# w1's last 64 rows: half by a transfer with an outermost dimension of 4, half by one of 16

## Chip, cores, metric

One core of one Trainium2 chip. The metric is the device time of one execution in microseconds (us), lower is better. Before: 213.92 us.

## The reference, cut to what matters

The result is the sum of the layernormed input, an attention block over a sliding window of a cache and a small MLP block. The change touches one product of the MLP block, `layernorm(x) @ w1`, with 576 rows of w1.

```python
def _B_ref(x, w1, w2, w3, w4):
    B, S, D = x.shape                      # 4, 1, 576
    h = _gelu(_layernorm(x, axis=-1) @ w1) # w1 is 576 x 576
    ...                                    # shifts, @ w2, residual, layernorm, @ w3, gelu, @ w4
x = A_x
xn = _layernorm(x, axis=-1)
return x + _A_ref(xn, ...) + _B_ref(xn, ...)
```

## The kernel before: the parts that matter

576 rows are 4 x 128 and a rest of 64. The 512 rows fill 128 partitions; the 64 of w1 lie in 16 partitions, 4 rows in each, and those of w2 in 32 partitions, 2 rows in each. One queue, SP's, loads all weights and the cache in a fixed order, about 88 MB.

```python
w1rag = w4_t[0:16, 18 * D:22 * D]
w2rag = w4_t[0:32, 22 * D:24 * D]
...
# order in the queue: w2, wq, wq/w3 rest ("wqr"), the two ragged pieces ("r12"), w3, w1, 16 K tiles, 8 V tiles, wo, w4
ev_r12 = add_dma([(w1rag, B_w1[512:576, :].rearrange("(b a c) n -> a b (c n)", b=4, a=4)),
                  (w2rag, B_w2[512:576, :].rearrange("(b a c) n -> a b (c n)", b=4, a=8))], "r12", (), -58.5)
ev_w3 = add_dma([(w3_t[:], B_w3[0:512, :].rearrange("(p r) n -> p (r n)", r=4))], "w3", (), -57)
...
# in ln_ops, second layernorm: the last 64 columns, in the order of the rows in w1rag
r_out = ragsrc[:, idx, 0:64].rearrange("q (c a b) -> q c a b", c=4, a=4)
r_in = r_in.rearrange("q (b a c) -> q c a b", b=4, a=4)
add("dve", lambda e: e.tensor_copy(out=r_out, in_=r_in), waits=[f"{tag}_n", "rag_zero"], sig=tag, key=k0 + 0.05)
...
# pe_h: 4 matmuls over 128 partitions, then 4 over 16
for c in range(4):
    ins = e.matmul(HTps[h], lhsT=xn2T[0:16, 4 + c, :], rhs=w1rag[:, c * D + HALF * h:c * D + HALF * (h + 1)], start=False, stop=(c == 3))
```

The outermost dimension of the HBM side, the source (4 for w1's rest, 8 for w2's), is there on purpose: a 4 went with 4 of the 16 DMA engines and an 8 with 8. In the trace of this kernel four strings of packets hold the packets of 4608 bytes of w1's rest, four in each, eight hold those of 2304 bytes of w2's, and the semaphore of the two gets 12 single updates, from 16.61 to 17.80 us: 4 and 8 engines. A semaphore is a counter; in the program each transfer adds 16 to it. In the trace that is several updates, for w3 16 of them from 27.44 to 28.73 us, and the matmuls that wait for w3 start at 28.78, after the last.

## Time and profile before

| | before |
|---|---|
| median of 6 runs, us (lowest, highest) | 213.92 (213.80, 214.04) |
| span of the traced run | 212.7 |
| DMA queue, share of 16 engines | 97.6% |
| last update of w3's semaphore | 28.73 |
| last update of the last piece of w4 | 210.47 |
| from there to the last update of the stores of the result | 2.20 |

PE is TensorE (PEld its weight loads), DVE VectorE, ACT ScalarE, POOL GpSimd; SP issues the transfers. The span is what the trace shows from the first to the last instruction; the device time is longer by about 1.3 us. In the timeline each line has the start, the length, the engine, the source line, the operation, and in brackets the idle time before it and what ended it.

### The profile page before, as it was taken

Reading aid. Unit: us, or ns where it says so; the run is one execution under the profiler, and the core shown is the slowest. Engines: PE = TensorE matmul, PEld = TensorE weight load, DVE = VectorE, ACT = ScalarE, POOL = GpSimd, SP = SyncE. Lnnn points to the kernel's source line nnn. Section 1 sums busy time; section 2 is a strip of 40 time slices with the busy share of each in tenths; the row PEclk is TensorE's granted clock in tenths of the full one; section 3 lists DMA queues with packets and bytes.
Section 4 is the critical chain, followed back from the end, with each engine's and each line's share of the span. In section 5 each row is a group of like instructions: output and inputs, shape, how many; then the busy total and the mean of one; then the engine's idle time right before and its main releaser. Section 6 shows DMA issues by size and latency. Waiting matters only on the chain. (4 is left out here: it accounts for less than half of the span.)

```text
span 212.7 us, 4936 instructions
## 1 busy us (share of the span) xinstructions
PE 169.3 (80%) x2171; PEld 131.9 (62%) x2171; DVE 106.6 (50%) x162; ACT 61.6 (29%) x76; POOL 15.4 (7%) x55
## 2 busy tenths in 40 slices
PE   0038359999999999999997095999999696779964
PEld 0013246888778887888874044888878575657532
DVE  0332700676766666666664429877776473600100
ACT  2001204566555666666666520000000000000000
POOL 8300000450000000000000000000000000000000
PEclk9999958999999999999999679999999999969999
DMA  7999999999999999999999999999999999999993
GB/s 290 414 390 467 437 401 431 425 433 410 434 431 428 425 428 438 421 425 434 422 450 456 404 434 438 413 462 410 431 441 419 425 450 419 449 409 421 429 407 119
DMA packets 5150, 88.65 MB, mean 417 GB/s; under 512 B 600, under 2 KB 740, under 8 KB 1300
## 3 DMA queue, kind: packets, MB, share of 16 engines
q1 hardware_dynamic: 5124, 88.49, 97.6%
q8 instruction: 8, 0.13, 0.2%
q14 instruction: 2, 0.02, 0.0%
q10 hardware_dynamic: 16, 0.01, 0.0%
HBM read 88.49 MB, written 0.00 MB: 416 GB/s over the span
## 5 line engine op out<-in xcount | busy, mean ns | idle before, releaser
L370 DVE COPY kt<-ps 128x1024 bf16<-128x1024 bf16 x80 | 52.3, 687 | 26.1 <-PE ps L363 25.9
L363 PEld LDWEIGHTS ps<-perm_bf,ring 128*128 128x128 bf16 x1024 | 57.5, 98 | 9.6 <-issue 9.2
L363 PE MATMUL ps<-perm_bf,ring 128*128 128x128 bf16 x1024 | 62.1, 219 | 0.8
L369 ACT ACTIVATE kt<-ps 128x1024 bf16<-128x1024 bf16 x48 | 48.8, 1023 | 30.1 <-PE ps L363 29.0
L441 DVE TENSOR_TENSOR kt<-PT,mU_bf 128x2048 bf16<-128x2048 bf16 x32 | 38.7, 1223 | 17.9 <-PE ps L452 17.9
L452 PE MATMUL ps<-ring,kt 128*128 128x256 bf16 x256 | 29.8, 280 | 5.1 <-PEq L621 5.1
L452 PE MATMUL ps<-w,kt 128*128 128x256 bf16 x256 | 28.4, 272 | 4.8 <-PEq L621 4.8
L452 PEld LDWEIGHTS ps<-ring,kt 128*128 128x128 bf16 x256 | 25.6, 100 | 9.2 <-issue 5.6
L452 PEld LDWEIGHTS ps<-w,kt 128*128 128x128 bf16 x256 | 24.8, 98 | 8.3 <-issue 5.5
L466 ACT ACTIVATE Ov<-ps 64x128 f32<-64x128 f32 x2 | 0.5, 272 | 68.2 <-PE ps L452 68.2
L377 PE MATMUL ps<-kt,Qs 128*32 128x512 bf16 x272 | 17.8, 382 | 1.4 <-PEq L621 1.4
L299 PE MATMUL ps<-ident_bf,xn_bf 4*128 4x4 bf16 x8 | 0.6, 170 | 12.7 <-DVE ragsrc L293 12.7
L398 POOL COPY Qs<-Qpad 128x128 bf16<-128x128 bf16 x16 | 4.6, 293 | 82.1 <-PE ps L377 68.2
L377 PEld LDWEIGHTS ps<-kt,Qs 128*32 128x32 bf16 x272 | 5.7, 95 | 6.8 <-issue 1.5
L416 PE MATMUL ps<-kt,sel 128*128 128x512 bf16 x16 | 5.0, 480 | 5.6 <-ACT kt L408 5.6
L299 PEld LDWEIGHTS ps<-ident_bf,xn_bf 4*128 4x128 bf16 x8 | 0.4, 112 | 12.7 <-issue 10.3
L560 PE MATMUL ps<-w,x1nT 128*32 128x387 bf16 (+7 forms) x90 | 5.8, 400 | 2.7 <-DMA w<-in_B_w_dram 2.5
L416 PEld LDWEIGHTS ps<-kt,sel 128*128 128x128 bf16 x16 | 1.8, 117 | 8.8 <-ACT kt L408 6.1
L560 PEld LDWEIGHTS ps<-w,x1nT 128*32 128x32 bf16 x90 | 4.5, 124 | 3.9 <-DMA w<-in_B_w_dram 2.6
L597 DVE CAST out_sb<-ps 4x288 bf16<-4x288 f32 x1 | 0.4, 445 | 12.7 <-PE ps L479 12.7
L466 DVE COPY Ov<-ps 64x128 f32<-64x128 f32 x2 | 0.6, 283 | 10.4 <-PE ps L452 10.4
L479 PE MATMUL ps<-w,h2T_sb 128*4 128x288 bf16 x54 | 3.6, 286 | 2.1 <-DMA w<-in_B_w_dram 2.1
(113 smaller groups left out, 73.7 us busy)
## 6 DMA issues: line engine op xcount, KB each, us to landing
ring<-in_A_k_cache_dram SPq DMA_DIRECT2D x16, 2048.0 KB, 14.4
w<-in_A_v_cache_dram SPq DMA_DIRECT2D x4, 4096.0 KB, 23.4
ring<-in_A_v_cache_dram SPq DMA_DIRECT2D x4, 4096.0 KB, 31.2
w<-in_B_w_dram SPq DMA_DIRECT2D x1, 4608.0 KB, 24.1
w<-in_A_wo_dram SPq DMA_DIRECT2D x1, 4608.0 KB, 32.0
kt<-in_A_wq_dram SPq DMA_DIRECT2D x1, 4096.0 KB, 13.1
w<-in_B_w_dram SPq DMA_DIRECT2D x1, 2592.0 KB, 29.2
w<-in_B_w_dram SPq DMA_DIRECT2D x3, 576.0 KB, 14.0
```

What stands on the lines that cost most here:

```text
L299: e.transpose(XTps[idx][:, r, :], v[:, r, :], ident_bf[0:B, 0:B])
L363: ins = e.transpose(tb[n % 4][:, t, :], slot_t(c)[:, 8 * k + t, :], perm_bf[:])
L369: return "act", lambda e: e.activation(out=ktbuf[:, n % 16], in_=tb[n % 4], func=ACTF.Copy)
L370: return "dve", lambda e: e.tensor_copy(out=ktbuf[:, n % 16], in_=tb[n % 4])
L377: ins = e.matmul(Sps[32 * u:32 * u + 32, q, :].rearrange("p (t i) -> p t i", t=16), lhsT=Qs[:, c % NPOS, 32 * u:32 * u + 32], rhs=ktgrp[:, ...
L398: P(lambda e, c=c, cc=cc: e.tensor_copy(out=Qs[:, c % NPOS, :], in_=Qpad_t[:, 128 * cc:128 * cc + 128]), waits=["qT", "qs_zero"] + ([f"SC{ ...
L416: ins = e.matmul(ps[:, 4 + g, :].rearrange("p (q t) -> p q t", q=4), lhsT=sel[:, g // 2, g % 2, i, :], rhs=P_v[:, i], start=(i == 0), stop ...
L441: return lambda e: e.tensor_tensor(out=pads[:, j], in0=PTv[:, b, q, VQ * j:VQ * (j + 1), :].unsqueeze(2).to_broadcast([128, VQ, 32, 2]), i ...
L452: ins = e.matmul(Ops, lhsT=pads[:, j, t:t + 2].rearrange("p t h e -> p (t h e)"), rhs=vslot[q][:, t0:t0 + 2 * Dh], start=(q == 0 and j == ...
L466: add(eng, (lambda e, o_=o_, i_=i_: e.activation(out=o_, in_=i_, func=ACTF.Copy)) if x else (lambda e, o_=o_, i_=i_: e.tensor_copy(out=o_, ...
L479: return e.matmul(ACC[h], lhsT=lhsT, rhs=rhs, start=start, stop=stop, tile_position=(0, 32 * h), skip_group_check=True)
L560: ins = e.matmul(H2ps[k][32 * g:32 * g + 32, :].rearrange("p (x c) -> p x c", c=9)[:, :, off:off + cnt], lhsT=x_, rhs=w[:, base_:base_ + 1 ...
```

## The change

Its intent is balance among the DMA engines. The four that carry all 64 rows have more bytes than the others (four packets of 4608 bytes more on each); half of the rows now go by all 16. A second copy on DVE puts the activations of that half into the matching order.

```diff
-        ev_r12 = add_dma([(w1rag, B_w1[512:576, :].rearrange("(b a c) n -> a b (c n)", b=4, a=4)),
+        ev_r12 = add_dma([(w1rag[:, 0:2 * D], B_w1[512:544, :].rearrange("(b a c) n -> a b (c n)", b=4, a=4)),
+                          (w1rag[:, 2 * D:4 * D], B_w1[544:576, :].rearrange("(p c) n -> p (c n)", c=2)),
                           (w2rag, B_w2[512:576, :].rearrange("(b a c) n -> a b (c n)", b=4, a=8))], "r12", (), -58.5)
...
             if idx == 1:
-                r_out = ragsrc[:, idx, 0:64].rearrange("q (c a b) -> q c a b", c=4, a=4)
-                r_in = r_in.rearrange("q (b a c) -> q c a b", b=4, a=4)
+                r_sp = r_in[:, 32:64].rearrange("q (p c) -> q c p", c=2)
+                add("dve", lambda e: e.tensor_copy(out=ragsrc[:, idx, 32:64].rearrange("q (c p) -> q c p", c=2), in_=r_sp),
+                    waits=[f"{tag}_n", "rag_zero"], sig=None, key=k0 + 0.045)
+                r_out = ragsrc[:, idx, 0:32].rearrange("q (c a b) -> q c a b", c=2, a=4)
+                r_in = r_in[:, 0:32].rearrange("q (b a c) -> q c a b", b=4, a=4)
```

## The prediction

> **What bounds the kernel now.** I read the page's summary of all engines first (parts 1 to 3), then the chain of work that ended last, then the timeline of the first 20 us, where the change lies, and last the packet and semaphore records under these views.
>
> ```profile
> span 212.7 us, 4936 instructions
> PE 169.3 (80%) x2171; PEld 131.9 (62%) x2171; DVE 106.6 (50%) x162; ACT 61.6 (29%) x76; POOL 15.4 (7%) x55
> ...
> DMA  7999999999999999999999999999999999999993
> ...
> q1 hardware_dynamic: 5124, 88.49, 97.6%
> q8 instruction: 8, 0.13, 0.2%
> q14 instruction: 2, 0.02, 0.0%
> ```
>
> No compute engine is full, but the 16 DMA engines are busy from the first slice to the last but one: 88.49 MB on one queue take 97.6% of 16 engines' span. The reader should also note the two small "instruction" rows: ten packets of program text that share these engines. They matter below.
>
> ```profile
> 177.53 7.16 PE ps L452 x64
> 184.69 0.02 issue
> 184.71 24.68 DMA ring<-in_B_w_dram
> 209.39 0.04 issue
> 209.43 1.42 PE ps L479 x18
> 210.85 0.43 DVE out_sb L597
> ```
>
> This is the chain that ended last, in order of time. Its last 28 us are the last w4 pieces coming through the DMA queue, 18 matmuls, one cast. The next line, from the timeline, shows that even within those matmuls the last two weight loads waited for the very last piece (2 weight loads at 210.52, idle before them ended by the DMA):
>
> ```profile
> 210.52 0.08 PEld L479 LDWEIGHTS ps<-ring,h2T_sb 128*4 128x4 bf16 x2 [0.26 <-DMA ring<-in_B_w_dram]
> ```
>
> So the time is: the start of the queue (first packet at 1.83 us), plus the work of the DMA engine that finishes last (the last semaphore update of the last piece is at 210.47), plus a tail of 2.2 us. The question of this change is therefore not how many bytes are moved, for they stay the same, but on which of the 16 engines.
>
> **The engines one by one.** The packet records give start, duration and size, not the engine; but each engine works without a gap, so its packets can be strung together. In the steady part a 16384-byte packet takes 611 ns and the next of the same engine starts 607 ns after it: 27.0 GB/s for each engine. Where 16 such strings run, all with the same sizes in the same order from w3 to the last piece of w4, the ends of the 16 differ only by what an engine did besides. In us, the end of the last packet of each, in order: 207.81, 207.84, 207.93, 208.14, 208.27, 208.89, 209.09, 209.41, 209.41, 209.44, 209.47, 209.54, 209.67, 209.71, 209.80, 210.03. The spread is 2.2 us, and only the last counts. Three things make the spread. (a) w1's last 64 rows: four engines show the four packets of 4608 bytes of this transfer, and start w3 at 17.18 to 17.47 where the other twelve start it at 16.20 to 16.67. (b) The 16 KB instruction packets of q8 (seven before the end, at 29.2, 40.1, 48.4, 118.0, 127.5, 144.5, 159.2): each holds up one engine by 1.5 us in all (for example 971 + 505 ns), and all seven engines are among the twelve. (c) The two 8 KB packets of q14 (46.2 and 87.5): they hold up two of the four by 0.96 and 0.68 us. The engine that ends last, at 210.03, is one of the four with w1's rows and had the 0.96; the next, at 209.80, 209.71 and 209.67, are of the twelve, with an instruction packet each.
>
> [...] the semaphore of the two ragged transfers gets two updates at 4.17 and 4.97, then 12 single ones from 16.61 to 17.80, that is 4 and 8 engines (dimensions 4 and 8).[...]
>
> **The change part by part.**
> Removed: one transfer of 73.7 KB, k = 4, four packets of 4608 bytes on each of four engines. Such a packet takes 178 ns and the next starts 174 after it; the semaphore packet takes about 6. So 4 x 174 + 6 = 702 ns on each of the four.
> Added: 32 rows with dimension 4, so 16 packets of 2304 bytes, four on each of the same four engines; the same size is in the trace (w2's ragged rows: 93 ns, 89 from start to start). 4 x 89 + 6 = 362 ns. And 32 rows with dimension 16: one such packet on each of the 16 engines, 89 + 6 = 95 ns.
> Net: the four have 362 + 95 - 702 = -245 ns, the twelve have +95 ns. The sum over 16 engines is +160 ns, 10 ns each: splitting costs practically nothing.
> At the end: the engine at 210.03 moves to 209.79. The leader of the twelve moves from 209.80 to 209.90 and is now the last. 209.90 - 210.03 = -0.13 us. From the semaphore updates of the last piece (210.47 the last, 210.21 the one before) it is 210.21 + 0.095 - 210.47 = -0.165 us. I take -0.15. Does the tail follow? The matmuls of the three last pieces start after 209.39, 210.11 and 210.47; at about 70 ns each the 16 of the first two need 1.1 us, to 210.5, about when the last piece lands. The first two pieces come earlier by the same 0.15, so they follow.
>
> Also added: one copy of 4 x 32 on DVE, and one more issue on SP. The lines that tell their cost:
>
> ```profile
> 12.72 0.20 DVE L293 COPY ragsrc<-xn_bf 4x64 bf16<-4x64 bf16 x1
> 12.98 0.20 PEld L299 LDWEIGHTS ps<-ident_bf,xn_bf 4*128 4x128 bf16 x4 [2.40 <-DVE ragsrc L293]
> ...
> 13.20 0.24 PE L303 MATMUL ps<-ident_bf,ragsrc 4*16 4x4 bf16 x4
> ...
> 14.44 3.60 PE L322 MATMUL ps<-kt,xnT 128*32 128x512 bf16 x32 [1.00 <-DMA kt<-in_A_wq_dram]
> ```
>
> The copy takes about 0.2 us and pushes the transposes from 12.98 to 13.2; they end at 13.6 instead of 13.44, and PE then waits anyway until wq lands, at 14.40. It disappears in the 1.00 us of idle time shown in the last line.
>
> ```profile
> 3.00 2.50 SPq L185 DMA_DIRECT2D w<-in_B_w_dram  x4
> 5.54 3.24 SPq L185 DMA_DIRECT2D ring<-in_A_k_cache_dram  x4
> ```
>
> An issue takes 2.50 / 4 = 0.6 us. w3, w1 and the first four K tiles are issued 0.6 us later, by 9.4 us instead of 8.8; the first packet of w3 starts at 16.2, so the queue does not run dry.
>
> **The rivals.**
> 1. The prologue is on the path: 0.2 (copy) + 0.6 (issue) would make 214.5 to 214.7. Against it: the idle 1.00 us, and the full queue.
> 2. Only the total of bytes counts (a shared limit behind the engines, which would give a relieved engine's time to the others): then 213.92 stays. Against it: packets of 611 ns repeat to the nanosecond on all 16, whoever has finished.
> 3. The instruction packets land on other engines, because DVE's and SP's programs are each longer by an instruction or so. A 1.5 us packet on one of the five early engines costs nothing (208.27 + 1.5 = 209.8); one on an undelayed engine of the four would give about 209.09 - 0.25 + 1.5 = 210.3, +0.3 us; two on one engine +1.3. If on the other hand the 0.96 us left the last engine, the twelve would still hold the end at 209.90. PE's program, the only long one, does not change, so I give this one in eight.
>
> **Range and chances.** 213.92 - 0.15 = 213.77 us. The three runs before lie within 0.15 of each other, and which engine is hit by what may move it by 0.1 to 0.4 either way, more upwards, since the eleven others of the twelve cap the gain. I give 213.55 to 214.1. Two per cent is 4.3 us; the whole spread of the engines is 2.2, so faster by 2% is out of reach, and slower by 2% needs a mechanism that I do not see. 0.5%, 98.5%, 1%.
>
> **What would show it.** Right: the ragged semaphore gets updates from 4, 16 and 8 engines; the four engines start w3 only about 0.7 us behind the twelve rather than 1.0; the 16 ends draw together, with the last one of the twelve; the wait on wq before 14.44 shrinks by 0.2 and its end stays; the last update of the last piece is near 210.3. Wrong: the first wq matmul later than 14.44; one of the four still last; instruction packets at other times or on other engines; or the last piece unmoved though the four were relieved.

k is the number of engines that carry a transfer. The 4 and the 8 come from the trace; that dimension 16 would bring 16 engines, and that w1's first half would stay on the same four, was my estimate from them. The "about 6" ns of a semaphore packet are from its start to that of the next packet; its record is 9 ns long.

## More of the kernel before

The page's lines that say what bounds the kernel are in the prediction. One line more will serve as a gauge later: the matmuls that wait for all of w3, so for the slowest DMA engine at that point.

```profile
28.78 1.48 PE L560 MATMUL ps<-w,x1nT 128*32 128x387 bf16 x21 [2.47 <-DMA w<-in_B_w_dram]
```

## The result, and the profile after

214.07 us, median of 6 runs (214.03 to 214.13), against 213.92 (213.80 to 214.04). The ratio is 1.0007, with a 95% interval of 0.9994 to 1.002: the same. ("The same" means within 2%.) Ratios here are the mean time of one kernel's runs over that of the other's of the same rounds, so not quite the ratio of the medians quoted. The predicted range, 213.55 to 214.1, holds the result, but the sign of the small shift is not the predicted one (213.77).

From the page of the changed kernel:

```profile
span 212.8 us, 4936 instructions
...
DMA  7999999999999999999999999999999999999993
...
q1 hardware_dynamic: 5156, 88.49, 97.7%
```

Same bytes, 32 packets more (5124 before), the same full queue. The end of the chain that ended last, in order of time:

```profile
184.71 24.69 DMA ring<-in_B_w_dram
209.40 0.04 issue
209.45 1.41 PE ps L483 x18
210.86 0.43 DVE out_sb L601
```

It stands where it stood (209.43 and 210.85 before). So the four engines that were relieved do not end the kernel earlier. The timeline of the changed kernel around the copy, and the gauge on w3:

```profile
13.77 0.17 DVE L293 COPY ragsrc<-xn_bf 4x32 bf16<-4x32 bf16 x1
13.86 0.17 DVE L297 COPY ragsrc<-xn_bf 4x32 bf16<-4x32 bf16 x1
14.08 0.29 PE L303 MATMUL ps<-ident_bf,xn_bf 4*128 4x4 bf16 x4 [2.38 <-DVE ragsrc L297]
14.30 0.24 PE L307 MATMUL ps<-ident_bf,ragsrc 4*16 4x4 bf16 x4
...
14.48 3.60 PE L326 MATMUL ps<-kt,xnT 128*32 128x512 bf16 x32
...
28.71 1.80 PE L564 MATMUL ps<-w,x1nT 128*32 128x387 bf16 x25 [1.80 <-DMA w<-in_B_w_dram]
```

The copies overlap, so the added one lengthens this chain by less than 0.1 us. The whole chain is 1.05 us later than before, because x landed at 9.11 us and not at 8.06. Still the first matmul on wq starts at 14.48 (14.44 before): the idle microsecond took it all. The last line is the first sign of where the gain went. By the packet sum, an estimate, w3 should be complete 0.245 us earlier for the four late engines, near 28.49; its last semaphore update is at 28.67, and these matmuls start 0.07 earlier, not 0.25. In second traces of both kernels the last update is at 28.77 before and 28.79 after: there nothing is gained.

The packet and semaphore records show why. These are not a view of the page; the numbers below are worked out from them as follows. "Lag": the mean time of the single semaphore updates less the mean start of the 4-byte packets, over 14.5 to 18 us, where the ragged rows come (44 updates and 44 such packets before, 60 and 60 after). "First w3 packet": the mean duration of the first packet of 36864 bytes on each of the 16 engines. "Mean" and "last": of the 16 updates of the last piece of w4. A second trace of each was taken in the experiments.

```
                          lag ns   first w3 packet ns   mean us   last us   last - mean   to the stores' end
before, two traces        344 345      1368 1372        209.48 209.48   210.47 210.51   0.99 1.03   2.20 2.20
changed, two traces       507 511      1428 1429        209.72 209.65   210.48 210.50   0.77 0.85   2.27 2.27
```

Read from right to left, this is the result. The last of the 16 engines is 0.20 us nearer to their mean (1.01 to 0.81), as was meant. But all 16 engines on the average end 0.20 us later, where the packet sum of the prediction had 0.01. In these traces the two cancel, and the last update stays. (The distance of the last from the mean is a weak measure: it is 0.83 in the run of two transfers with dimension 4 below, where nothing was relieved.) A tail that is longer by 0.07 us remains. The first two columns say where the 0.2 comes from: while the ragged rows are written, completions lag by 165 ns more, and the next packet of an engine takes 60 ns more on the average (1371 to 1508 in the first trace, 1364 to 1408 before). The w2 rests, 93 ns each before, are at 99 on the average with the new packets, and by w3's landing the mean of the 16 is already later by 0.18 (27.91 to 28.09). The 16 engines begin w3 at the same time on the average (16.65 before, 16.63 after, two traces each), so the loss lies in w3's own stretch: its first packets take the 60 ns, and the lag of w3 and w1, worked out in the same way, is 392 ns before and 489 after. From the K tiles on it is 480 to 488 in all four traces.

### The profile page after: what moved, and what is told of

Same layout as the page of the kernel before. It is cut to its first block, busy times and chain, and to the rows that moved or that the text cites. A ratio compares the mean times of both kernels' runs of the same rounds, so it can differ in the third digit from the quotient of the medians.

```text
span 212.8 us, 4936 instructions
## 1 busy us (share of the span) xinstructions
PE 170.9 (80%) x2169; PEld 132.7 (62%) x2171; DVE 106.8 (50%) x163; ACT 61.8 (29%) x76; POOL 15.4 (7%) x55
## 5 line engine op out<-in xcount | busy, mean ns | idle before, releaser
L456 PE MATMUL ps<-w,kt 128*128 128x256 bf16 x256 | 29.8, 281 | 3.0 <-PEq L625 3.0
L456 PE MATMUL ps<-ring,kt 128*128 128x256 bf16 x256 | 28.4, 273 | 4.3 <-PEq L625 4.3
L456 PEld LDWEIGHTS ps<-w,kt 128*128 128x128 bf16 x256 | 25.7, 101 | 7.0 <-issue 3.4
L456 PEld LDWEIGHTS ps<-ring,kt 128*128 128x128 bf16 x256 | 24.9, 98 | 7.7 <-issue 4.8
L420 PE MATMUL ps<-kt,sel 128*128 128x512 bf16 x16 | 6.3, 576 | 5.6 <-ACT kt L412 5.6
L483 PE MATMUL ps<-w,ORT 128*4 128x288 bf16 x64 | 4.1, 286 | 1.7 <-DMA w<-in_A_wo_dram 1.7
```

The lines of the kernel that those rows point to most:

```text
L420: ins = e.matmul(ps[:, 4 + g, :].rearrange("p (q t) -> p q t", q=4), lhsT=sel[:, g // 2, g % 2, i, :], rhs=P_v[:, i], start=(i == 0), stop ...
L456: ins = e.matmul(Ops, lhsT=pads[:, j, t:t + 2].rearrange("p t h e -> p (t h e)"), rhs=vslot[q][:, t0:t0 + 2 * Dh], start=(q == 0 and j == ...
L483: return e.matmul(ACC[h], lhsT=lhsT, rhs=rhs, start=start, stop=stop, tile_position=(0, 32 * h), skip_group_check=True)
```

## The experiments

Theories. **Crowding**: the new transfer sends 16 engines into 16 neighbouring partitions, and they get into each other's way there (lag 507 ns), more than the 4 engines of the old form (344). By what they would do so is not shown, and no record shows which engine writes where. In the expectations the name that this theory had is cut, with the unmeasured mechanism behind it; what stands right after such a cut, before the source theory or an "if", is what crowding predicts. **Source**: 16 engines read one small stretch of HBM at once. **Prologue**: the added issue, the added copy or the later x cost the time. **Chance**: single traces differ by as much.

The twelve runs follow, in the order in which they ran; four, four, three and one shared a chip and the runs of the kernel before. The record marks all of them as correct, the ones with a wrong result too, so its check does not see these rows; that a version computes the right thing is read from its edit.

**The kernel before, again.** No edit.

> Control: the kernel before against itself, for a second trace and the width of the noise. Both theories: ratio 1.000. If the ends of the 16 DMA engines are fixed by the program, the last packet ends at 210.03 us again, the next at 209.80, and the last engine is again one of the four with w1's rows; if they differ by 0.2 us or more between two traces of one program, a change of 0.15 us cannot be read from single traces. w3's first packets (36864 bytes) take 1364 to 1370 ns again if that is of the program, or up to 1430 as in the trace of after if it is chance.

213.90 us, ratio 0.9997 (0.9984 to 1.0011). The lag, the first packets and the mean repeat to within a few ns and 0.01 us; the last update moved by 0.04. The two traces of the changed kernel differ more in the mean, by 0.07. So the mean can carry a verdict on a tenth or two, not on less. Single times cannot: 5 runs of this one program ran from 213.79 to 214.09 us.

**The changed kernel, again.** No edit.

> The changed kernel a second time. Theory A (the twelve other engines now hold the end, and the new 16-engine transfer also slows the packets around it): 214.05 to 214.1 us, ratio 1.0005 to 1.001, the last engine one of the twelve, w3's first packets again at about 1430 ns instead of 1366. Theory B (chance of a session): ratio within 0.0003 of 1 and w3's first packets at 1366 ns.

214.09 us, ratio 1.0006 (0.9992 to 1.0019). Lag 511 and first packets 1429 ns: of the program, not chance. The last engine is one of the twelve, at 210.09, with an instruction packet at 49 us. In this run x landed at 8.02 us, so the late x of the first trace was chance, and without consequence: the time is the same. The timeline of this run at that place:

```profile
13.21 0.24 PE L307 MATMUL ps<-ident_bf,ragsrc 4*16 4x4 bf16 x4
14.39 1.05 PE L326 MATMUL ps<-kt,xnT 128*32 128x512 bf16 x8 [0.93 <-DMA kt<-in_A_wq_dram]
```

**Two transfers, both with dimension 4**: all by-products of the change without its point.

```diff
-(w1rag[:, 2 * D:4 * D], B_w1[544:576, :].rearrange("(p c) n -> p (c n)", c=2)),
+(w1rag[:, 2 * D:4 * D], B_w1[544:576, :].rearrange("(b a c) n -> a b (c n)", b=4, a=4)),
```

(and the copy's order to match)

> All the by-products of the change, without its point: two transfers of 32 rows, both with outermost dimension 4, the second copy on DVE and the third issue on SP. Theory A (what counts is which engines carry the rows): 4 x 89 + 6, twice, is 724 ns on each of the four instead of 702, so +0.02 us on the engine that is last: 213.94, ratio 1.0001, w3's first packets at 1366 ns, the last engine one of the four. Theory C (the extra issue, the extra copy or the later landing of x costs the time): as the changed kernel, 214.05 to 214.1.

213.92 us, ratio 1.0001 (0.9988 to 1.0015), with x at 9.07 us. Lag 347, first packets 1364 on all 16. The added issue, the added copy, the smaller packets and a late x together cost nothing that shows. The prologue falls. Note the mean, 209.54, and the last update, 210.37: with nothing relieved, the last update is 0.10 to 0.14 earlier than in the two traces of the kernel before. So much it moves without any relief.

**All 64 rows by dimension 16**, one transfer, one copy.

```diff
-(w1rag, B_w1[512:576, :].rearrange("(b a c) n -> a b (c n)", b=4, a=4)),
+(w1rag, B_w1[512:576, :].rearrange("(p c) n -> p (c n)", c=4)),
```

(and the copy's order to match)

> The other end: all 64 rows by one transfer with outermost dimension 16, no added issue and no added copy. By packet times alone the four are relieved by 702 - 180 = 522 ns and each of the twelve gets 4608 bytes, 174 + 6 = 180 ns: the leader of the twelve goes from 209.80 to 209.98, so -0.05 us, 213.87. Theory A with disturbance by a transfer of 16 engines: another 0.1 to 0.2 us, 214.0 to 214.1, and w3's first packets again well over 1366 ns. Theory C: as the kernel before or faster, 213.87 or less, since issue and copy are as there, and x lands at 8.1 us.

214.64 us, ratio 1.0032 (1.0018 to 1.0045): the clearest effect, and well above what I expected. Lag 731 ns, first w3 packets 1853 ns, mean 210.22 (+0.74), last 211.12. The cost is more than proportional: twice the bytes of the change, 3.7 times the rise of the mean. The gauge on w3 in its timeline:

```profile
29.21 1.15 PE L560 MATMUL ps<-w,x1nT 128*32 128x387 bf16 x15 [2.56 <-DMA w<-in_B_w_dram]
```

and the end of its chain of work, in order of time:

```profile
210.10 1.40 PE ps L479 x18
211.50 0.43 DVE out_sb L597
```

The chain ends 0.65 us later than before (209.43, 210.85). The matmuls that wait for w3 start 0.43 us later (29.21 and 28.78) although by the packet sum, an estimate, the four late engines had 0.52 us less to do.

**The same 16 engines, other partitions** (wrong result: the matmul reads zeros for most of these rows).

```diff
-(w1rag, B_w1[512:576, :].rearrange("(p c) n -> p (c n)", c=4)),
+(w4_t[0:128:2, 18 * D:19 * D], B_w1[512:576, :]),
```

(and zeros in `w1rag`, written by POOL before the transfer is issued)

> All 64 rows on 16 engines again[...], but written one row to each of 64 partitions (0, 2, ... 126) instead of 4 rows to each of the 16 partitions 0 to 15. Wrong result on purpose: the matmul reads zeros instead of these rows. Packets are 4 of 1152 bytes, 47 ns each, and 6: 194 ns on each engine. [...] the crowding is gone, w3's first packets at 1364 to 1375 ns, leader of the twelve 209.80 + 0.19 = 209.99, so -0.04 us, 213.9. Source theory (16 engines reading one small stretch of HBM at once): w3's first packets again about 1850 ns, 214.5 to 214.7.

The crowding is gone: lag 345, first packets 1364 on all 16, mean 209.52. The gauge on w3:

```profile
28.21 2.15 PE L561 MATMUL ps<-w,x1nT 128*32 128x387 bf16 x31 [1.75 <-DMA w<-in_B_w_dram]
```

28.21 against 29.21: one whole microsecond between two kernels whose 16 engines carry the same number of bytes each, in all the same 64 rows, and where the packets put it (28.78 - 0.51 = 28.27, to within 0.06). The source theory wanted 1850 ns here. Two reservations: the packets are of 1152 bytes, not 4608, and the last update, 210.45, is no better than before. The time, 214.10, ratio 1.0011 (0.9996 to 1.0026), looks worse than the trace; the device time exceeds the span by 1.40 us in its runs, 1.24 to 1.32 in most others, so 0.1 of it lies outside the span, and I do not know why. By the span it is 212.73 on the average, against 212.62 of the kernel before in the same rounds.

**The same partitions, another source** (wrong result).

```diff
-(w1rag, B_w1[512:576, :].rearrange("(p c) n -> p (c n)", c=4)),
+(w1rag, B_w1[0:512, :].rearrange("(p s) n -> p (s n)", p=16)[:, 0:4 * D]),
```

> All 64 rows' worth of bytes on 16 engines into partitions 0 to 15 as in the run where all rows came that way, but each engine's 4608 bytes are read 36864 bytes apart, from w1's first 512 rows. Wrong result on purpose. [...] nothing changes, w3's first packets 1800 to 1900 ns, 214.5 to 214.8. Source theory: w3's first packets near 1366, 213.87.

214.64 us, ratio 1.0036 (1.002 to 1.0051), the time of the run with all rows by 16. The gauge:

```profile
29.10 1.29 PE L560 MATMUL ps<-w,x1nT 128*32 128x387 bf16 x16 [2.48 <-DMA w<-in_B_w_dram]
```

Lag 608 and first packets 1688 ns are a little below the 731 and 1853 with neighbouring rows, mean 210.12 against 210.22. So the source has a small part at most (0.09 us of the 0.74 in the mean); the destination makes the effect. The prediction of "1800 to 1900" was missed by that part.

**The change, with the second half spread over partitions 0, 4, ... 124** (wrong result).

```diff
-(w1rag[:, 2 * D:4 * D], B_w1[544:576, :].rearrange("(p c) n -> p (c n)", c=2)),
+(w4_t[0:128:4, 20 * D:21 * D], B_w1[544:576, :]),
```

(and zeros in the second half of `w1rag`, written by POOL first)

> The change itself, 32 rows by 4 and 32 by 16 engines, but the second half written to partitions 0, 4, ... 124, one row each. Wrong result on purpose (these rows count as zero). Packets: four of 2304 bytes and two of 1152 on each of the four, 362 + 100 - 702 = -240 ns; +100 on each of the twelve. [...] w3's first packets at 1364 to 1375 instead of 1428, no other slowing, so what the prediction worked out holds: last packet at 209.90, last update near 210.32, 213.79 us, ratio 0.9993. Source theory, or slowing by the third transfer as such: as the changed kernel, last update at 210.48, 214.05 to 214.1.

A miss for the end: last update 210.48, not 210.32. The disturbance did go as expected: first packets 1373 ns, lag 375, mean 209.53, so 0.05 above before and not 0.2. And the gauge on w3 is as early as the packets have it (28.78 - 0.24 = 28.54; the three traces without relief have 28.75 to 28.81):

```profile
28.50 1.80 PE L565 MATMUL ps<-w,x1nT 128*32 128x387 bf16 x25 [1.65 <-DMA w<-in_B_w_dram]
```

So at w3 the relief of the four is there without crowding, and not with it (28.71 and 28.84 in the changed kernel). But at the end the last engine, one of the twelve with an instruction packet, was late all the same (210.06). Freedom from crowding did not by itself bring the predicted gain. 214.13 us, ratio 1.0014 (1.0 to 1.0027), again with more time outside the span (1.53 us; one run of 214.63 with a span of 212.7 makes part of it, the other four have 1.41 to 1.45); spans 212.66 on the average, 212.62 before.

**Meant for 8 engines, but 16 came.** 32 rows into 32 partitions, one row each, correct result.

```diff
+w1ragb = w4_t[0:32, 20 * D:21 * D]
-(w1rag[:, 2 * D:4 * D], B_w1[544:576, :].rearrange("(p c) n -> p (c n)", c=2)),
+(w1ragb, B_w1[544:576, :].rearrange("(a b) n -> a b n", a=8)),
```

(and one matmul over 32 partitions in place of two over 16)

> A correct version[...]: 32 rows by 4 engines as in the change, the other 32 by 8 engines into 32 partitions, one row each[...]. The four: 362 + 194 - 702 = -146 ns; the next four engines +194; the other eight unchanged. Last packet: 209.89 on the four, 209.80 on the eight, 209.86 to 209.90 on the next four: 209.9, that is -0.13 us, 213.79, ratio 0.9994; w3's first packets at 1364 to 1375. If a third transfer costs time by itself: 213.95 or more.

My own error in the edit. The 8 groups of 4 rows are contiguous in HBM; they were merged into one dimension of 32, as the list of the built instructions shows (32x576 where w2's transfer stands as 32x1x1152). The queue has 5172 packets, 48 more than before: with four packets of half the size on each of the four, 32 more with data and 16 more for semaphores. And the semaphore got two early updates, not three; those on 4 and 8 engines had one each before the change, so this one was on 16. It became a useful step in between: 16 engines into 32 neighbouring partitions, not 16. Lag 444, first packets 1373, mean 209.65, last update 210.43; 214.09 us, ratio 1.0012 (0.9999 to 1.0026). Beside the run before it this is a clean pair: the same rows by the same number of engines, packets of 1152 bytes in both, only the partitions differ (0 to 31, or 0, 4, ... 124): lag 444 against 375, mean 209.65 against 209.53. So the smaller packets are not what removed the crowding. What it is about neighbouring partitions that crowds, no run shows.

**Really 8 engines** into the same 32 partitions, 4 rows by each, correct result. ("There" in the expectation is the run before.)

```diff
-(w1ragb, B_w1[544:576, :].rearrange("(a b) n -> a b n", a=8)),
+(w1ragb, B_w1[544:576, :].rearrange("(b a) n -> a b n", a=8)),
```

(and the copy's order to match)

> [...] there the eight groups of rows were contiguous in HBM, were merged into one dimension of 32 and went by 16 engines[...]. Here the rows are taken 8 apart, so that the dimension of 8 stays[...]. Correct result. The four: 362 + 194 - 702 = -146 ns; the next four +194; the other eight 0. [...] completion of the ragged stage lags its semaphore packets by about 345 ns as in the kernel before (444 in the run with 32 partitions and 16 engines, 509 in the changed kernel), mean landing of the last piece 209.48 to 209.53, the last update 210.3 to 210.4. Time 213.8 to 213.9, but one run scatters by 0.2. If any third transfer that relieves the four costs time: mean landing 209.65 or more and 214.05 or more.

The queue has 5164 packets, 40 more than before: 32 with data, 8 for semaphores. In the trace all goes as the crowding theory has it: lag 343, mean 209.44, last update 210.31, span 212.5. (The run of two transfers with dimension 4 had 210.37, without any relief.) The timed runs do not follow: 213.83 to 214.30, median 214.09, ratio 1.0011 (0.9998 to 1.0025).

**48 rows by dimension 4, 16 by dimension 16**, correct result.

```diff
-(w1rag[:, 0:2 * D], B_w1[512:544, :].rearrange("(b a c) n -> a b (c n)", b=4, a=4)),
-(w1rag[:, 2 * D:4 * D], B_w1[544:576, :].rearrange("(p c) n -> p (c n)", c=2)),
+(w1rag[:, 0:3 * D], B_w1[512:560, :].rearrange("(b a c) n -> a b (c n)", b=4, a=4)),
+(w1rag[:, 3 * D:4 * D], B_w1[560:576, :]),
```

(and the copies to match)

> The change with another size: 48 rows by 4 engines, 16 rows by 16, one row to each of partitions 0 to 15. Correct result. Packets of 3456 bytes, about 132 ns by the two sizes beside it: four of them and 6, and 47 + 6: -116 ns on the four, +53 on the twelve. [...] half the crowded bytes of the changed kernel, so the mean landing of the last piece rises by less than half of its 0.2 us, to 209.50 to 209.57; last update 210.35 to 210.45; 213.85 to 213.95. If the crowding were not dosed by bytes: 209.65 to 209.7 as in the changed kernel.

213.91 us, ratio 1.0002 (0.9989 to 1.0016). Lag 404, mean 209.59 (0.11 above before, expected 0.02 to 0.09), last update 210.50 (expected up to 210.45). The dose holds in order: with 18, 37 and 74 KB by 16 engines into partitions 0 to 15 the lag is 404, 509 and 731 and the mean rises by 0.11, 0.20 and 0.74.

**The change without its 16-engine transfer** (wrong result: the first 32 rows are read twice).

```diff
-(w1rag[:, 2 * D:4 * D], B_w1[544:576, :].rearrange("(p c) n -> p (c n)", c=2)),
...
-rhs=w1rag[:, c * D + HALF * h:c * D + HALF * (h + 1)]
+rhs=w1rag[:, c % 2 * D + HALF * h:c % 2 * D + HALF * (h + 1)]
```

> The changed kernel without its transfer by 16 engines: the last 32 rows are not loaded at all and the matmul reads the first 32 a second time. Wrong result on purpose. The four: 362 - 702 = -340 ns, the twelve 0; no crowding. Mean landing of the last piece 209.48 - 0.085 = 209.40; the twelve cap the gain, so the last update goes from 210.47 to 210.2 to 210.3, -0.2 us, 213.7. If relief of the four does nothing for the end: 213.92.

In the trace: lag 338, mean 209.39 (expected 209.40), last update 210.17, span 212.4, so -0.3. In time: median 213.78, ratio 0.9999 (0.9986 to 1.0013). The chain's last two lines in this trace:

```profile
209.14 1.40 PE ps L482 x18
210.55 0.43 DVE out_sb L600
```

That is 0.3 us earlier than before. But the five runs' spans are 212.4, 212.6, 212.8, 212.5 and 212.5: a gain between none and 0.3, in a kernel that moves less. On the four the relief is larger than the change's (0.34 us for 0.245), with nothing added to the twelve. The mean of the 16 fell by 0.09, the share of the four in it: what they were spared was not given to the others.

**Really 8 engines, once more.**

> The same correct kernel (32 rows by 4 engines, 32 by 8 engines[...]) once more, because its trace (last update 210.31, span 212.5) and its timed runs (213.83 to 214.30) did not agree. If the relief of the four is worth what the packets say: about 213.8, ratio 0.9995, and last updates near 210.3 again. If the trace was a lucky one and this version is no faster: 214.0 to 214.1, ratio 1.0005 to 1.001.

213.88 us, ratio 1.0007 (0.9994 to 1.0021). The trace again has lag 349, mean 209.47, last 210.28, span 212.5; the other four runs have spans up to 212.9. No gain is shown. No version beats the kernel before of the same rounds: the only one with a lower median there computes less.

One more fact of all the traces: the tail from the last update of w4 to that of the result's stores is 2.27 or 2.28 us in every kernel with a 16-engine transfer into neighbouring partitions (six traces of five kernels), and 2.19 or 2.20 in all others. The packets of the two stores interleave differently: those of one start at 212.06 to 212.13 and of the other at 212.16 to 212.24 before, but at 212.07 to 212.21 and 212.11 to 212.24 in the first trace of the changed kernel. What links this to a transfer 195 us earlier is open.

## Why the prediction was right or wrong, point by point

- **The bound and its reading, right.** The queue is full throughout and the DMA engine that ends last sets the end. When all rows went by 16 engines and every engine ended later by 0.74 us on the average, the time went up by 0.72.
- **Number of engines, right.** 4, 16 and 8 show in the semaphore: in the changed kernel two early updates (for 4 and 8, at 4.15 and 5.40 us), then 28 single ones (16.45 to 17.77).
- **"The sum over 16 engines is +160 ns, 10 ns each: splitting costs practically nothing", wrong.** This is the step that failed. The mean of the 16 went up by 0.20 us. I took the duration of a 2304-byte packet from a transfer of 8 engines into 32 partitions, and put it into one of 16 engines into 16. Of its own packets little shows (99 for 93 ns); it is the packet behind (1428 for 1368) and the completions (lag 509 for 345, then 489 for 392 in w3 and w1) that pay.
- **The relief of the four, right; its worth at the end not shown.** The prediction's own sign came: the four start w3 0.68 and 0.66 us after the twelve on the average, against 0.92 and 1.02 before, and the last engine is one of the twelve. The distance of the last from the mean shrank by 0.20 us, but by nearly as much (0.18) without relief in the run of two transfers with dimension 4. The sum on the leader of the twelve was mis-sized: +0.095 worked out, but 209.80 to 210.05 in the first pair of traces, +0.25.
- **-0.15 us at the end, wrong.** The result lies in the range of 213.55 to 214.1, at its upper end and on the other side of 213.92; that is luck, since the range was made for engines hit by chance and a second error of 0.2 us happened to cancel the gain. Last update +0.01 and 0.00; then the tail, which I took to follow unchanged, +0.07. Device time +0.15 with an interval of ratios that includes 1. Over all runs the kernel before has a mean of 213.89 (47 runs, standard deviation 0.11) and the changed one of 214.07 (11 runs, 0.05); these are of several chips and only a hint that a loss of 0.1 to 0.2 is real. The traces account for 0.07 to 0.1 of it (spans 212.70 and 212.74, then 212.78 and 212.80).
- **Would it have held without crowding?** Not shown. The run with the second half spread, and the two runs with 8 engines, have the mean within 0.05 of before, yet only the traces of the latter end earlier (210.3), and their timed runs do not. The starts of the engines at the head of the queue differ from run to run by a tenth or two, and so does the one that is last.
- **Rival 1, prologue: rightly rejected**, as the run of two transfers with dimension 4 shows; the late x, which I had not foreseen, was hidden as well. The added copy cost under 0.1 us, not the 0.2 I allowed.
- **Rival 2, only the total counts: wrong as such**, but the outcome looked like it. With the same bytes in all, 64 rows on 16 engines took 214.64 us into partitions 0 to 15 and 214.10 spread. The prediction's argument against it was too strong, though: packets of 16384 bytes do not repeat to the nanosecond. 611 ns is the commonest duration before (712 of 2048; 615 after, with 479), but in the K tiles most take 612 to 624.
- **Rival 3, instruction packets on other engines: no sign.** In the first trace they come at about the same times (29.7, 39.3, 48.0, 118.3, 127.7, 147.3, 161.4); in the second, where every engine can be followed, the seven large ones fall on seven of the twelve and the two small ones on two of the four, as before.
- **Chances.** 98.5% for "same" was right: the spread among the engines bounded what balance could do.

## What to carry to other kernels

Count the bytes of each DMA engine, but ask also where they land: here a small transfer on all 16 engines crowded 16 neighbouring partitions, and the large transfer behind it paid, on the average of all engines (0.11, 0.20 and 0.74 us for 18, 37 and 74 KB). Do not carry a packet's cost from one transfer to another with another share of engines to partitions; fewer engines into more partitions did not crowd here (8 into 32: lag 343 and 349 ns, against 509 for 16 into 16). And where a change is worth a tenth of a microsecond, look at a mean over engines that repeats (here to 0.01 and 0.07), not at the maximum or at one time.
